# The third group's second matmul in seven half products, with its helpers moved to other engines and places

## The chip, the cores and the metric

The kernel runs on one core of a Trainium2 chip. The metric is the device time of one execution in microseconds, the median of three runs. A profile is of one such execution: its span is counted from the first to the last instruction that the profiler saw, and lies a little below the time of the same execution.

## The reference

The input x has 8 sequences of 4224 tokens with 192 channels. First comes a causal convolution over tokens with 7 taps; the taps are a softmax of a weight per head, and each of 8 heads has 24 channels. Its result is normalised per token and goes through two matrix products with a ReLU between them, and is added to that product.

```python
w = softmax(weight)                                   # (8 heads, 7 taps)
out = einsum('hk,bskhg->bshg', w, windows_of(x, 7))   # causal, padded with zeros
mu, var = out.mean(-1), out.var(-1)
xn = (out - mu) / sqrt(var + 1e-6) * g_ln
y = out + maximum(xn @ w_ch1, 0) @ w_ch2              # 192 -> 768 -> 192
```

All is in float32 (the two weight matrices arrive as doubles and are put together from their two words on the chip).

## The kernel before

**Groups.** Each of the 128 partitions holds tokens, and the tokens are cut into 18 groups: group 0 has 6 tokens per partition, group 1 has 8 (the left over tokens of all sequences), group 2 has 10, and groups 3 to 17 have 16 each. The list `groups` stands on line 70. All order is written out by hand; each engine runs its instructions in the order of the program, and waits are put in where data asks for them.

**What happens to a group g.** `load_x` (L132) brings x into one of two buffers. `first_tap` (L369) writes tap 0 times x to y on ScalarE. From group 4 on, `second_tap` (L382) writes tap 1 times x to a tile tb, also on ScalarE, and two transfers on the POOL queue (L392) add tb to y in memory, an accumulating transfer for each half of the tokens. `conv` (L397) adds the other taps on VectorE, an instruction per tap and head (L403). `transpose` (L408) brings y to channel-major form in yt, 32 x 32 blocks at a time. `moments` (L425) takes mean and variance per token (L434), and `root` (L436) makes 1/sqrt(var) of them with 19 small instructions on GpSimd. `store_y` (L472) writes y to the output, where `add_to_out` (L886) later adds the scaled second product by accumulating transfers on the POOL queue.

**The two products.** The first product, `up` (L525), and the second, `down` (L738), use 32-wide tiles of TensorE, four at a time. For groups 0 to 2 each is done in full: 144 matrix products, two instructions each. From group 3 on both are cut into halves along both dimensions and done in seven half products with sums before and after (Winograd's form of Strassen's algorithm): `up_mixed` (L587) and `down_fast` (L789). That needs sums of the quarters of w1 and w2 (`sums_of_quarters`, L555), sums of the quarters of yt (`sums_of_y`, L569, two on VectorE and two on GpSimd), and half sums of the hidden tile between the products (`half_sum`, L770, and `lower_sum`, L777). `product` (L801) is one half product: for three column blocks, 12 matrix products each, then a copy from PSUM by ScalarE (L812), and then the next few pieces of other ScalarE work from the list `work`.

**Order around the change.** The loop over groups (L973) does for g = 0, 1, 2: load of x for g + 2, `up(g)`, taps and transpose of group g + 1 on VectorE, the first taps of g + 2, `down(g)`, and `park(g)` (ScalarE copies the product out of PSUM, L870). At g = 1 it also finishes group 0 and 1 (`finish`, L919, transposes back), makes the roots of groups 0 to 2 (L1005, L1008), and all four sums of w2 on VectorE (L1006). At g = 2 VectorE makes the four sums of w1 (L1012) and the sums of yt for group 3 (L1013). While `up(2)` runs, ScalarE scales groups 0 and 1 (L884) and the POOL queue adds them to the output. The hidden tile is one large room in SBUF, shared by all groups; a group of fewer tokens uses the first part of it in the full form.

In `down_fast`, the first four half products need only the hidden tile, `lower_sum` and two sums of w2. Then VectorE makes three triples of half sums, (1,1), (0,0) and (0,1), which the last three half products read. The first triple can start when the third product has been read.

Of the kernel before, what the change touches and what calls it, by code (L numbers as in the profile page):

```python
# [16 lines left out]
def kernel(  # L17
# [59 lines left out]
    fast[NG - 1] = J - 5  # L77
    NFAST = max(fast.values())
# [53 lines left out]
    def load_x(g, queue=nc.sync):  # L132
# [3 lines left out]
        flat = t.rearrange("p j d -> p (j d)")  # L136
        if b is None:
# [14 lines left out]
        if b:  # L152
# [7 lines left out]
            nc.gpsimd.memset(t[0:1, 0:PAD, :], 0.0)  # L160
# [221 lines left out]
    def second_tap(g, heads=(0, H)):  # L382

        n = groups[g][2]
        if heads[0] == 0:
            tb[g] = bpool.tile([P, J, D], F32, tag="tb", name=f"tb{g}")
# [3 lines left out]
        if heads[1] == H:  # L390
            for j1, j2 in ((0, n // 2), (n // 2, n)):
                nc.gpsimd.dma_start(  # L392
                    out=y[g][:, j1:j2].rearrange("p j d -> p (j d)"),
                    in_=tb[g][:, j1:j2].rearrange("p j d -> p (j d)"), accum_op=ALU.add,
                )
# [99 lines left out]
    def evict_up(g, f, src):  # L495
# [4 lines left out]
        elif width(g) == C:  # L500
            dst = ht[g][:, :, f // FC, f % FC].rearrange("p h q j t -> p q h (j t)")
# [22 lines left out]

    def up(g):  # L525
# [3 lines left out]
        scaled = (0, 1) if g == 2 else ()  # L529
        hidden_tile(g)  # L530
        for f in range(NF):
# [8 lines left out]
            if 1 <= f <= 4:  # L540
                for s in scaled:
                    m = groups[s][2]
                    scale(s, m * (f - 1) // 4, m * f // 4)
                    if f % 2 == 0:
                        add_to_out(s, m * (f - 2) // 4, m * f // 4)


# [7 lines left out]
    def sums_of_quarters(dst, b11, b12, b21, b22):  # L555
        d0, d1, d2, d3 = dst
        for v, a, b in ((d2, b12, b22), (d0, b12, b11), (d1, b22, d0), (d3, b21, d1)):
            nc.vector.tensor_tensor(v, a, b, op=ALU.subtract)
# [28 lines left out]
    def up_mixed(g, ahead, pending):  # L587
# [79 lines left out]
        next(ahead)  # L667

# [120 lines left out]
    def down_fast(g, work):  # L789
# [32 lines left out]
        if g + 2 < NG:  # L822
# [4 lines left out]
        product(0, a[:, 0, 0], b[0], c11, True, 3)  # L827
        product(1, a[:, 1, 0], w2sums[:, 2], c22, True, 2)
        product(1, a[:, 1, 1], w2sums[:, 3], c21, False, 2)
        product(1, a[:, 0, 1], b[2], None, True, 3)  # L830
        if g + 1 < NG:
            transpose(g + 1)
        half_sum(g, (1, 1), (1, 1), (1, 0), ALU.add)
# [12 lines left out]
        if g + 1 < NG:  # L846
            sums_of_y(g + 1, nc.gpsimd)
            moments(g + 1)
        else:
            finish_fast(g, 0, flat, cs, parts)  # L850
# [35 lines left out]
    def add_to_out(g, j1, j2):  # L886
# [3 lines left out]
        for ps, rows in rows_of_out(g, j1, j2) if j2 else ():  # L890
            nc.gpsimd.dma_start(  # L891
# [166 lines left out]
```

## Time and profile before

| | us |
|---|---|
| median of 3 runs | 962.1 (960.88 to 962.82) |
| the profiled execution | 960.25 |
| its span | 958.5 |
| TensorE busy / VectorE busy / ScalarE busy / GpSimd busy | 948.6 / 895.8 / 686.6 / 260.9 |
| second product of group 0, 1, 2 in the chain of waits | 11.84, 15.68, 19.52 |
| second product of groups 3 to 16, each | 27.44 |
| first product of groups 3 to 16, each | 27.96 |

The busy time of an engine is the time in which at least one of its instructions runs. The chain of waits is found from the last instruction backwards: at each step it names what that instruction waited for. What stands in it has set the end; what does not stand in it was hidden. A group of instructions has its line in the kernel, the engine, the operation, the tile written and the tile read, the shapes, and a mean duration; consecutive instructions of one engine overlap a little, so their pace is read from a stretch of the timeline, as its length over their count.

### The profile page before, as it was taken

What the parts mean: (1) busy time and instruction counts of PE and PEld (TensorE: products, weight loads), DVE (VectorE), ACT (ScalarE), POOL (GpSimd) and SP (SyncE); (2) the same over time, 40 slices, a digit from 0 to 9 for tenths busy, and PEclk for the clock granted to TensorE, in tenths of its full rate; (3) what the DMA queues carried; (4) which work ended last, traced back from release to release, by engine and by line L of the source; (5) the groups of instructions that cost most, each with busy time, mean ns of one, the idle gap of its engine ahead of it and who ended that gap; (6) DMA issues with size and microseconds to landing.
All of it is one profiled execution on the core that took longest, in us unless ns stands there. A gap on an engine that the chain in (4) does not pass through costs nothing.

```text
span 958.5 us, 38499 instructions
## 1 busy us (share of the span) xinstructions
PE 948.6 (99%) x17274; PEld 719.5 (75%) x17274; DVE 895.8 (93%) x1510; ACT 686.6 (72%) x1139; POOL 260.9 (27%) x399
## 2 busy tenths in 40 slices
PE   8999999999999999999999999999999999999997
PEld 7886596776869687786958678686867768586787
DVE  8999998999999999999999999999989999999667
ACT  6625578596877959687796958778695877866461
POOL 1005311612135131422216131341315221161400
PEclk9999999999999999999999999999999999999999
DMA  8243887679697887969788796978879697767241
GB/s 221 79 155 112 180 207 216 146 151 265 134 260 142 235 173 158 249 123 276 136 240 163 178 234 118 281 136 243 158 186 216 120 280 141 179 132 129 53 83 68
DMA packets 28394, 166.69 MB, mean 174 GB/s; under 512 B 3397, under 2 KB 4294, under 8 KB 22215
## 3 DMA queue, kind: packets, MB, share of 16 engines
q0 software_dynamic: 21568, 100.94, 55.0%
q1 hardware_dynamic: 6656, 63.31, 17.9%
q8 instruction: 135, 2.21, 0.9%
q14 instruction: 29, 0.24, 0.1%
q10 hardware_dynamic: 6, 0.00, 0.0%
HBM read 38.93 MB, written 50.33 MB: 93 GB/s over the span
## 4 chain that ended last, share of the span: by engine, by line
PE 97%; ACT 1%; DMA 1%; DVE 0%; SPq 0%; issue 0%; ACTq 0%
PE ps L519 48%; PE ps L806 42%; PE ps L753 6%; DMA xg<-in_x_dram 1%; PE ps L322 1%; ACT w L360 0%; ACT room L618 0%; DVE y L898 0%; ACT spare L241 0%; ACT y L378 0%; PE ps L335 0%; SPq L215 0%; ACT room L509 0%; PE ps L350 0%; SPq L210 0%
## 5 line engine op out<-in xcount | busy, mean ns | idle before, releaser
L403 DVE SCALAR_TENSOR_TENSOR y<-xg,taps,y 128x384 f32<-128x384 f32 (+3 forms) x734 | 367.9, 577 | 1.8 <-issue 1.6
L519 PE MATMUL ps<-yt,w 32*128 32x256 f32 (+2 forms) x4104 | 235.7, 379 | 0.4 <-ACT room L509 0.4
L806 PE MATMUL ps<-room,w2sums 128*32 128x256 f32 (+1 forms) x4320 | 235.9, 375 | 0.0
L618 ACT COPY room<-ps 128x1024 f32<-128x1024 f32 (+1 forms) x135 | 175.0, 1296 | 77.2 <-PE ps L519 76.0
L519 PEld LDWEIGHTS ps<-yt,w 32*128 32x128 f32 x4104 | 204.2, 185 | 26.5 <-issue 9.0
L806 PEld LDWEIGHTS ps<-room,w2sums 128*32 128x32 f32 x4320 | 140.5, 110 | 89.7 <-ACT room L631 4.9
L806 PE MATMUL ps<-room,w 128*32 128x256 f32 (+1 forms) x3240 | 181.0, 375 | 0.4 <-issue 0.4
L773 DVE TENSOR_TENSOR room<-room 128x1024 f32<-128x1024 f32 (+1 forms) x135 | 151.6, 1196 | 21.2 <-PE ps L806 20.0
L806 PEld LDWEIGHTS ps<-room,w 128*32 128x32 f32 x3240 | 104.8, 110 | 68.7 <-DVE room L624 5.0
L519 PE MATMUL ps<-ysums,w1sums 32*128 32x256 f32 x2160 | 124.9, 379 | 0.0
L519 PEld LDWEIGHTS ps<-ysums,w1sums 32*128 32x128 f32 x2160 | 108.7, 185 | 11.2 <-ACT room L618 3.6
L812 ACT COPY cs<-ps 128x256 f32<-128x256 f32 (+1 forms) x180 | 66.0, 369 | 42.6 <-PE ps L806 42.6
L884 ACT ACTIVATE ot<-ot,r 128x192 f32<-128x192 f32 x232 | 93.8, 462 | 0.0
L631 ACT ACTIVATE room<-room 128x1024 f32<-128x1024 f32 (+1 forms) x89 | 92.1, 1071 | 0.0
L891 POOL DMA_DIRECT2D out_dram<-ot x40 | 34.2, 1086 | 194.6 <-ACT ot L884 115.7
L378 ACT ACTIVATE y<-xg,taps 128x384 f32<-128x384 f32 (+3 forms) x141 | 72.8, 611 | 9.0 <-DVE st L434 7.6
L434 DVE BATCH_NORM_STATS2 st<-y 128x6 f32<-128x192 f32 x264 | 70.2, 344 | 0.0
L519 PE MATMUL ps<-yt,w1sums 32*128 32x256 f32 x1080 | 65.1, 379 | 0.0
L812 ACT COPY room<-ps 128x256 f32<-128x256 f32 (+1 forms) x90 | 33.6, 373 | 43.9 <-PE ps L806 42.4
L519 PE MATMUL ps<-ysums,w 32*128 32x256 f32 x1080 | 64.5, 376 | 0.0
L618 ACT ACTIVATE room<-ps 128x1024 f32<-128x1024 f32 (+1 forms) x30 | 43.6, 1454 | 27.6 <-PE ps L519 27.6
L389 ACT ACTIVATE tb<-xg,taps 128x384 f32<-128x384 f32 x112 | 61.9, 635 | 0.0
(109 smaller groups left out, 895.3 us busy)
## 6 DMA issues: line engine op xcount, KB each, us to landing
xg<-in_x_dram SPq DMA_DIRECT2D x15, 2112.0 KB, 19.2
room<-room POOLq DMA_DIRECT2D x45, 512.0 KB, 5.3
out_dram<-ot POOLq DMA_DIRECT2D x29, 768.0 KB, 9.5
y<-tb POOLq DMA_DIRECT2D x28, 768.0 KB, 11.4
out_dram<-y SPq DMA_DIRECT2D x13, 1536.0 KB, 10.8
room<-parts_cs POOLq DMA_DIRECT2D x28, 512.0 KB, 6.6
room<-parts_tb POOLq DMA_DIRECT2D x14, 1024.0 KB, 7.6
xg<-in_x_dram SPq DMA_DIRECT2D x1, 1536.0 KB, 8.0
```

The costliest lines, as they stand in the source:

```text
L378: nc.scalar.mul(y[g][:, 0:n, cs], xg[g][:, 0:n, cs], taps[:, h, 0:1])
L389: nc.scalar.mul(tb[g][:, 0:n, cs], xg[g][:, 1 : 1 + n, cs], taps[:, h, 1:2])
L403: nc.vector.scalar_tensor_tensor(out=y[g][:, 0:n, cs], in0=t[:, k : k + n, cs], scalar=taps[:, h, k : k + 1], in1=y[g][:, 0:n, cs], op0=AL ...
L434: nc.vector.bn_stats(out=sums[g][:, j, :], in_=y[g][:, j, :])
L519: nc.tensor.matmul(banks[:, q, i * w : i * w + w], right[rows, c, P * i : P * i + P], left[rows, :, c, :], start=(first and c == 0 and i = ...
L618: nc.scalar.activation(dst, src, AF.Relu) if relu else nc.scalar.copy(dst, src)
L631: nc.scalar.activation(c, c, AF.Relu)
L753: nc.tensor.matmul(bank[C * q : C * q + C, 0:w], w2[:, f, C * c : C * c + C], left, start=(f == 0), stop=(f == NF - 1),)
L773: nc.vector.tensor_tensor(a[:, *dst, f], a[:, *left, f], a[:, *right, f], op=op)
L806: nc.tensor.matmul(dst[C * q : C * q + C, 0:w], right[:, f, C * c : C * c + C], left[:, f, q], start=(first and f == PAIR), stop=(f == PAI ...
L812: nc.scalar.copy(to[:, c], dst[:, 0:w].rearrange("p (j t) -> p j t", t=t))
L884: nc.scalar.mul(ots[g][:, j, :], ots[g][:, j, :], rstd[g][:, j : j + 1])
```

## The change

Group 2 (10 tokens) now has `fast[2] = 10`: its second product goes through `down_fast`, in seven half products whose tiles are 160 columns wide, where `down` used 320. Its first product stays as it was, but its result goes to the quarters of the hidden tile. With that come:

- Group 2 gets a second tap on ScalarE and accumulating transfers (three, of 4, 4 and 2 tokens), and VectorE's taps of it start at tap 2. Its tb lies in the tile ys.
- Group 3 gets a second tap for six of the eight heads. Its tb lies in the last part of the shared room, so it has to be read before `up(2)` fills that part; the four transfers move pieces of 144 channels. VectorE's taps of group 3 are cut into four stretches.
- The sums of w1 and w2 go from VectorE to GpSimd, each let in by a small memset on VectorE (`let_in`) that stands where transposes or moments follow. Only one sum of w1 stays on VectorE.
- All accumulating transfers of y and of the output, in all groups but group 1's output, move four tokens each (`add_second_tap`, `add_to_out`), where they moved half a group.
- The load of x for group 3 is issued before the stores of y of group 1, that of group 4 from the POOL queue, and that of group 5 behind a memset in `down_fast(2)`.
- The root of group 2 runs inside the first product of group 3; `store_y(3)` is issued there too. Scaling of groups 0 and 1 and the taps of groups 3 and 4 on ScalarE are placed between the evictions by a function `between`.

```diff
+    fast[2] = groups[2][2]
...
-    def load_x(g, queue=nc.sync):
+    def load_x(g, queue=nc.sync, pad=True, gate=False):
...
+        if gate:
+            nc.vector.memset(t[0:1, 0:1, 0:1], 0.0)
...
+        elif g == 2:
+            part = upool.tile([P, 3 * HJ * CH * C], F32, tag="ys", name="tb2")
+            tb[g] = part[:, 0 : n * D].rearrange("p (j d) -> p j d", d=D)
+        elif g == 3:
+            tb[g] = room[:, (NF * NQ * C - D) * J :].rearrange("p (j d) -> p j d", d=D)
...
-            for j1, j2 in ((0, n // 2), (n // 2, n)):
-                nc.gpsimd.dma_start(
-                    out=y[g][:, j1:j2].rearrange("p j d -> p (j d)"),
-                    in_=tb[g][:, j1:j2].rearrange("p j d -> p (j d)"), accum_op=ALU.add,
-                )
+            add_second_tap(g)
+
+    def add_second_tap(g, upto=H):
+        n = groups[g][2]
+        for js in (slice(j, min(j + 4, n)) for j in range(0, n, 4)):
+            ends = [v[:, js, 0 : upto * GRP] for v in (y[g], tb[g])]
+            if upto == H:
+                ends = [v.rearrange("p j d -> p (j d)") for v in ends]
+            nc.gpsimd.dma_start(out=ends[0], in_=ends[1], accum_op=ALU.add)
...
+    def between(g, f):
+
+        if g == 1 and f > 2:
+            second_tap(3, heads=[(0, 2), (2, 5), (5, 6)][f - 3])
+        elif g == 2:
+            if f == 0:
+                scale(0, 0, groups[0][2])
+                add_to_out(0, 0, groups[0][2])
+                nc.gpsimd.memset(xg[4][0:1, 0:PAD, :], 0.0)
+            elif f < 3:
+                m = groups[1][2]
+                scale(1, m * (f - 1) // 2, m * f // 2)
+                if f == 2:
+                    add_to_out(1, 0, m)
+            else:
+                first_tap(4, heads=[(0, 3), (3, 6), (6, 7)][f - 3])
...
-    def sums_of_quarters(dst, b11, b12, b21, b22):
-        d0, d1, d2, d3 = dst
-        for v, a, b in ((d2, b12, b22), (d0, b12, b11), (d1, b22, d0), (d3, b21, d1)):
-            nc.vector.tensor_tensor(v, a, b, op=ALU.subtract)
+    def let_in(tile):
+
+        nc.vector.memset(tile[0:1, 0:1, 0:1], 0.0)
+
+    def sums_of_quarters(dst, a, b):
+        nc.gpsimd.tensor_tensor(dst, a, b, op=ALU.subtract)
...
         next(ahead)
+        if g == 3:
+            store_y(g, nc.gpsimd)
...
+        behind = (1, 1, 1, 1) if g == 2 else (3, 2, 2, 3)
...
             transpose(g + 1)
+            if g == 2:
+                b11, b12 = quarters_of_w1()[0:2]
+                nc.vector.tensor_tensor(b12, b12, b11, op=ALU.subtract)
...
             sums_of_y(g + 1, nc.gpsimd)
+            if g == 2:
+                load_x(5, gate=True)
             moments(g + 1)
...
+            step = 4 * D if groups[g][0] is not None else (j2 - j1) * D
+            for d0 in range(0, (j2 - j1) * D, step):
+                d1 = min(d0 + step, (j2 - j1) * D)
+                nc.gpsimd.dma_start(out=rows[:, d0:d1], in_=src[:, d0:d1], accum_op=ALU.add)
...
-    results, pending = None, iter(())
+    results, pending = None, root(2)
...
-        if g + 2 < NG:
+        if g + 2 < NG and g not in (1, 2, 3):
             load_x(g + 2)
...
+        if g == 0:
+            early = CH * C // GRP
+            conv(1, heads=(0, early))
+            transpose(1, 0, CH)
+            conv(1, heads=(early, H))
+            transpose(1, CH, NC)
+            load_x(3)
+            store_y(1)
+            let_in(w1sums[:, 1])
+            moments(0)
+            moments(1)
+            first_tap(2)
+            second_tap(2)
+            sums_of_quarters(w1sums[:, 1], w12, w22)
+            sums_of_quarters(w2sums[:, 2], b12, b22)
+            next(root(0, True))
+        elif g == 1:
+            conv(2, 2)
+            transpose(2)
+            store_y(2)
+            first_tap(3)
+            add_second_tap(3, 6)
+            let_in(w1sums[:, 0])
+            sums_of_quarters(w1sums[:, 0], w11, w1sums[:, 1])
+            load_x(4, nc.gpsimd, pad=False)
+        elif g == 2:
+            conv(3, 2, 5, heads=(0, 6))
+            lower_sum(2)
+            conv(3, 5, K, heads=(0, 6))
+            let_in(w1sums[:, 2])
+            sums_of_quarters(w1sums[:, 2], w21, w1sums[:, 0])
+        if g < 2:
             down(g)
             park(g)
             if g == 1:
+                moments(2)
                 finish(0)
+                conv(3, heads=(6, H))
+                let_in(w2sums[:, 0])
                 finish(1)
+                sums_of_quarters(w2sums[:, 0], b12, b11)
+                sums_of_quarters(w2sums[:, 1], b22, w2sums[:, 0])
+                sums_of_quarters(w2sums[:, 3], b21, w2sums[:, 1])
             continue
```

On VectorE the order from group 1's last transpose on is thus: moments of groups 0 and 1, 40 taps of group 2, its transpose, moments of group 2, group 0's transposes back, 12 taps of group 3, group 1's transposes back, 18 taps, three lower sums of group 2, 12 taps, the transpose of group 3, the sum of w1, nine half sums, three additions, two sums of yt, moments of group 3.

## The prediction

> **What bounds the kernel now.** I read the totals of the engines first, then the chain of waits in order of time, then the timelines of VectorE, ScalarE and the two DMA queues from 20 to 190 us, and last the groups of instructions by shape, for prices.
>
> ```profile
> PE 948.6 (99%) x17274; PEld 719.5 (75%) x17274; DVE 895.8 (93%) x1510; ACT 686.6 (72%) x1139; POOL 260.9 (27%) x399
> PE 97%; ACT 1%; DMA 1%; DVE 0%; SPq 0%; issue 0%; ACTq 0%
> ```
>
> The chain itself, with start, length and instruction:
>
> ```profile
> 64.84 15.68 PE ps L753 x288
> 80.52 19.59 PE ps L519 x288
> 100.11 19.52 PE ps L753 x288
> 119.63 27.82 PE ps L519 x504
> 147.45 27.44 PE ps L806 x504
> ```
>
> TensorE is 97% of the chain, and from 31 us on its stages follow each other without a gap. So time is won only by less TensorE work, and each wait that reaches TensorE is lost in full. The third group's second product is the piece of 19.52 us at 100.11. VectorE is the engine that can spoil a gain:
>
> ```profile
> 49.39 1.62 DVE L434 BATCH_NORM_STATS2 st<-y 128x6 f32<-128x192 f32 x6
> 50.92 18.28 DVE L403 SCALAR_TENSOR_TENSOR y<-xg,taps,y 128x240 f32<-128x240 f32 x48
> 69.31 2.18 DVE L414 STREAM_TRANSPOSE yt<-y 128x1920 f32<-128x1920 f32 x1
> 81.36 25.49 DVE L403 SCALAR_TENSOR_TENSOR y<-xg,taps,y 128x384 f32<-128x384 f32 x48
> 159.04 10.31 DVE L773 TENSOR_TENSOR room<-room 128x1024 f32<-128x1024 f32 x9 [1.05 <-PE ps L806]
> ```
>
> These rows are start, time, engine, line. VectorE runs without idle time from 31.6 to 143.5 us; a step gives 18.28/48 = 0.381 us per tap of 240, 25.49/48 = 0.531 per tap of 384. The last row is the half sums of a seven-product group: they start when the third product ends, and the fifth product needs the first three.
>
> **What the Trainium skill says.** (1) "DMA: Bandwidth & Descriptors", section "Queues, rings and completion order": each DMA engine goes round between its queues and drains a whole packet of descriptors before it switches. The trace agrees: a store issued by SP at 154.53 moves nothing until 158.9, when the eight 6144-byte pieces per engine of an earlier POOL transfer are through. (2) "SBUF — State Buffer", "Who interferes with whom": a GpSimd instruction that reads SBUF and a VectorE instruction with two SBUF inputs exclude each other for a whole instruction; one with a single input does not contend. The trace shows the harmless half: the 768-element sums on POOL take 1.83 us beside the moments, whose pace stays 0.26. (3) "GPSIMD Engine Reference", "Side-by-side cycle accounting": tensor_tensor is 1.96 times slower there; here 1832 against 949 ns, 1.93. (4) "DMA: Bandwidth & Descriptors", "Why small descriptors are slow (HBM only)": between SBUF and SBUF small pieces aren't penalised. No run here shows pieces of 576 bytes.
>
> **The change part by part.**
>
> *TensorE.* Removed: 288 matmul instructions of 320 columns, 19.52 us. Added: 7 x 72 = 504 of 160 columns. The last group has this shape:
>
> ```profile
> L753 PE MATMUL ps<-room,w 128*32 128x160 f32 x288 | 10.0, 299 | 0.0
> L581 POOL TENSOR_TENSOR ysums<-yt 128x768 f32<-128x768 f32 x14 | 25.6, 1832 | 44.4 <-PE ps L806 39.5 <-DVE ysums L580 5.0
> L576 DVE TENSOR_TENSOR ysums<-yt 128x768 f32<-128x768 f32 x15 | 14.2, 949 | 0.0
> ```
>
> The 10.0 us there hold waits at its end; in its even stretch a bank of 48 took 1.63 us, 0.0340 each. 504 x 0.0340 = 17.14 us; saved 2.38. One product is 2.45 us, so with no wait the fifth starts at 100.11 + 4 x 2.45 = 109.90, and the next group at 117.25 instead of 119.63. No other TensorE work changes.
>
> *VectorE, if no transfer is late.* From 49.39: 14 moments at 0.26 = 3.66, 53.05. Forty taps of 240 (eight went to ScalarE and an accumulating transfer) 15.3, 68.4; transpose 2.1, 70.5; 10 moments 2.6, 73.1; group 0's transposes 1.6, 74.7; 12 taps of 384 6.35, 81.05; group 1's transposes 2.05, 83.1; 18 taps 9.5, 92.6; three half sums of 640 (1.135 us at 1024 and 0.80 at 704 give 0.735) 2.2, 94.8; 12 taps 6.35, 101.2; transpose 3.3, 104.5; one sum of 1152 1.4, 105.95. The third product ends at 107.4, so VectorE has 1.45 us in hand, and some 0.2 more because three half sums (2.2) are shorter than a product (2.45). After that: nine half sums, three additions of about 0.25, two of 0.95 bring it to about 117; 16 moments and the finish of group 2 (3.9) let group 4's taps begin near 125.2, 7.9 us after TensorE's start of the group, against 6.3 before and 7.05 in the steady groups. The product that is closed at 145.0 waited 1.46 us for TensorE before, which covers that.
>
> *ScalarE.* Added: 8 taps of 240 (3.1 us, 41.1 to 44.2; the copies it pushes back have until 49.1), six second taps of group 3 between the evictions of group 1 (0.53 each, they fill gaps of 1.57), 18 short copies for 6. In the seven products it does a copy of some 0.2 and a tap of 0.52 per 0.82 us: nothing. Group 4's first tap at 95 needs x of group 4, now loaded from POOL's queue behind a sum; I get it landed and padded near 91.
>
> *POOL's sums.* Three of 1152 (1.83 x 1152/768 = 2.75 us) and four of 288 (about 0.8). Where they fall beside moments and transposes they cost nothing; beside taps VectorE waits up to a whole sum. The second of 1152 stands behind four DMA issues that wait for ScalarE until 70.65 (0.55 us apart in the trace): 72.9 to 75.6, so 0.9 us of taps are held if VectorE is on time, none if it is 1 us late. The three sums of w2 (2.4 us) overhang group 1's transposes (2.05) by 0.3.
>
> *Group 2's new accumulating transfer.* This is the price that decides. ScalarE's taps end at 44.25; an accumulating transfer moved its first piece 1.4 us after issue (834.1 to 835.5), so 45.7. Three transfers: twice 8 pieces of 3072 bytes per engine (0.263 each, between 0.196 for 2304 and 0.340 for 4096) and 8 of 1536 (0.139): 2.1 + 2.1 + 1.1, ending at 51.2. But x of group 3 moves:
>
> ```profile
> 48.48 5.00 SPq L475 DMA_DIRECT2D out_dram<-y  x8
> 53.58 0.37 SPq L148 DMA_DIRECT2D xg<-in_x_dram  x1
> ```
>
> SP issued the stores first; now the load goes at 48.48 and its eight pieces per engine of 0.629 us (5.0) arrive at 49.4, while the second transfer is being drained (until 49.9). By (1) the load comes before the third transfer: 49.9 + 5.0 + 1.1 = 56.0, and 0.5 to be seen: VectorE's taps start at 56.5, not 53.05. Bounds: nothing if the three are drained first; 58.5 if the stores behind the load go ahead too. I take 3.5 us of lateness.
>
> *Sum.* 3.5 + 0.3 of late VectorE = 3.8: the half sums start at 109.75, three end at 112.0, the fifth product at 112.05 instead of 109.90, a wait of 2.15. Span 958.5 - 2.38 + 2.15 = 958.3; with the 1.75 us around the span (960.25 - 958.5) 960.0. The median of the runs shown, 962.1, is 1.85 above that execution, so I forecast 961.9.
>
> *Four tokens at a time.* y and out transfers double in number: four more issues per group, 2.2 us of a POOL that is 27% busy. Pieces of 3072 cost 2 x 0.263 where 6144 cost 0.479, 0.75 us more per 1.5 MB. In the steady groups y's transfers land 3 to 4 us before their taps, so nothing; if that cover were gone, up to 1.5 us a group. The later load of group 5 (near 117, used after 145), the root of group 2 (POOL, 121 to 131, read at about 136) and the later store of y of group 3 are hidden.
>
> **Rivals.** A: the wait goes out at about the old level (above), 961.9. B: the three transfers are drained before the load; VectorE is late by about 1.2 (POOL's sums), within its 1.65: the whole 2.38 stays, 959.8. For it: they are issued 4 us ahead. Against: the trace's switch at 158.9. C, slower: group 3's transfer from the shared tile goes in pieces of 576 bytes, 2048 pieces or 128 per engine. A line through 1536 to 8192 bytes gives some 0.078 us a piece, 10 us, landed near 84 with a store between: VectorE wants it at 86.6. The price of a 1536-byte piece, 0.139, is the upper bound: landed at 72.1 + 17.8 + 2.5 = 92.4, lateness 9.3, wait 7.6, 967.3. It decides from 0.115 a piece (landed at 89.3: slower by 2.0). Below: the price can't fall under the 0.036 at which the line meets zero bytes, and then A stands.
>
> **How the numbers follow.** A measurement here can tell 0.2%, 1.92 us, from no change. A 0.47, B 0.31, C with lesser late stalls of its sign 0.22. A reaches from 960.3 to 963.5, nearly all within 0.2%, a little on each side; B mostly beyond it. Range 959.4 to 965.0. Faster 0.33, within 0.2% 0.42, slower 0.25.
>
> **What would show it.** In the changed profile: 504 instructions of 160 columns at 0.034 us; a wait of VectorE before the first tap of 240 of 3 to 4 us, ended by the transfer from tb; a gap of about 2 us before the fifth product, released by the half sums; POOL's sum of 1152 beside moments. Wrong, if TensorE shows no gap near 110 (B), if group 3's taps wait at 87 (C), or if steady groups gain gaps.

## The result and the profile after

| | before | after |
|---|---|---|
| median over the runs of one comparison, us | 960.8 (959.7 to 962.9, 22 runs) | 962.5 (961.3 to 966.6, 22 runs) |
| ratio after to before, 95% interval | | 1.0019 (1.0011 to 1.0026) |
| profiled execution, its span, us | 960.25, 958.5 | 963.98, 962.1 |
| TensorE's stages: second product of group 2 | 19.52 | 19.03 |
| first product of group 3 | 27.82 | 28.07 |
| second product of group 3 | 27.44 | 30.53 |

The kernel became 1.7 us slower by the medians of the two. The three stages are measured from the start of a stage's first matrix product to the start of the next stage's, in the two profiled executions. They add up to 2.85 us more. Every later stage is equal (27.96 and 27.44 us), but for four stages that start between 676 and 761 us and are 0.2 to 0.6 us longer, since TensorE stalls in them; the kernel before has such a stage too (0.95 us longer, from 646), and they fall differently in each kernel's profiled execution. The profiled execution after lies above its median, so its span shows more than the medians do.

The totals of the engines and the shares of the chain, by engine, of the changed kernel:

```profile
PE 948.9 (99%) x17490; PEld 725.1 (75%) x17490; DVE 894.9 (93%) x1510; ACT 696.0 (72%) x1165; POOL 340.5 (35%) x473
PE 92%; DMA 3%; ACT 2%; POOL 1%; DVE 1%; issue 0%; SPq 0%; ACTq 0%; POOLq 0%; DVEq 0%
```

TensorE's share of the chain has fallen from 97% to 92%: other engines now release it somewhere. TensorE's own timeline of group 2's second product shows the first of these places (start, time, engine, line, tiles, shape and count; in brackets the idle time before it and what ended it):

```profile
99.94 2.65 PE L834 MATMUL ps<-room,w 128*32 128x160 f32 x72
102.41 5.07 PE L834 MATMUL ps<-room,w2sums 128*32 128x160 f32 x144
107.30 2.63 PE L834 MATMUL ps<-room,w 128*32 128x160 f32 x72
111.43 5.17 PE L834 MATMUL ps<-room,w2sums 128*32 128x160 f32 x144 [1.50 <-DVE room L801]
```

Four products take 2.45 us each, as expected, and then TensorE is idle for 1.50 us until VectorE's half sums are there; from matrix product to matrix product the gap is 1.80 us. VectorE's timeline, from group 2's taps to the half sums:

```profile
53.35 15.26 DVE L418 SCALAR_TENSOR_TENSOR y<-xg,taps,y 128x240 f32<-128x240 f32 x40 [0.32 <-DMA y<-tb]
...
75.02 8.82 DVE L418 SCALAR_TENSOR_TENSOR y<-xg,taps,y 128x384 f32<-128x384 f32 x12
...
85.77 10.13 DVE L418 SCALAR_TENSOR_TENSOR y<-xg,taps,y 128x384 f32<-128x384 f32 x18
...
107.86 1.32 DVE L867 TENSOR_TENSOR w<-w 128x1152 f32<-128x1152 f32 x1
109.10 6.70 DVE L801 TENSOR_TENSOR room<-room 128x640 f32<-128x640 f32 x9
```

Group 2's taps waited only 0.32 us for their accumulating transfers. But 12 taps of group 3 took 8.82 us where 12 others take 6.4, and 18 took 10.13 where 9.6 is their pace. At that time POOL did this:

```profile
69.67 5.24 POOL L410 DMA_DIRECT2D y<-room  x4 [9.71 <-ACT y L382]
72.78 4.81 POOL L584 TENSOR_TENSOR w1sums<-w,w1sums 128x1152 f32<-128x1152 f32 x1
```

The four issues with pieces of 576 bytes took 1.31 us each, so the sum of w1 behind them came to run beside the taps. One tap of the twelve took 3.00 us (their median is 0.605). The difference is nearly the length of the sum by itself, 2.65 us.

The second place is group 3's second product. These are POOL's queue, then ScalarE's timeline, then the chain there (start, length, what):

```profile
133.85 0.89 POOL L611 DMA_DIRECT2D room<-room  x1
134.45 0.85 POOL L490 DMA_DIRECT2D out_dram<-y  x1
135.37 1.79 POOL L611 DMA_DIRECT2D room<-parts_cs  x2
```

```profile
145.80 1.06 ACT L657 ACTIVATE room<-room 128x1024 f32<-128x1024 f32 x1 [2.08 <-DMA room<-parts_cs]
148.91 1.06 ACT L657 ACTIVATE room<-room 128x1024 f32<-128x1024 f32 x1 [2.05 <-DMA room<-parts_cs]
149.87 1.86 ACT L644 ACTIVATE room<-ps 128x2048 f32<-128x2048 f32 x1
```

```profile
133.37 0.44 POOL r L484
133.85 2.44 DMA room<-room
136.29 12.60 DMA room<-parts_cs
149.01 0.85 issue
149.87 1.86 ACT room L644
```

Read from the end: TensorE's second product waits for ScalarE's copy of the last first product (149.87). That copy stands behind two ReLUs (L657) that wait for the accumulating transfers of parts_cs. These were issued at 135.37, right behind the store of y of group 3, which moves 12288 bytes per partition on the same queue from 138 to 141.9; and the store stands behind a transfer issued at 133.85, late because the small instructions of the root of group 2 were still running in front of it. The root's last instruction (`POOL r L484`) and the transfer stand next to each other in the chain.

### The profile page after: what moved, and what is told of

Its sections match the earlier page's. It is cut to its first block, busy times and chain, and to the rows that moved or that the text cites. A ratio compares the mean times of both kernels' runs of the same rounds, so it can differ in the third digit from the quotient of the medians.

```text
span 962.1 us, 39172 instructions
## 1 busy us (share of the span) xinstructions
PE 948.9 (99%) x17490; PEld 725.1 (75%) x17490; DVE 894.9 (93%) x1510; ACT 696.0 (72%) x1165; POOL 340.5 (35%) x473
## 4 chain that ended last, share of the span: by engine, by line
PE 92%; DMA 3%; ACT 2%; POOL 1%; DVE 1%; issue 0%; SPq 0%; ACTq 0%; POOLq 0%; DVEq 0%
PE ps L534 45%; PE ps L834 43%; PE ps L781 4%; DMA room<-parts_cs 1%; DMA xg<-in_x_dram 1%; PE ps L369 1%; ACT room L644 1%; ACT room L657 0%; SPq L142 0%; DMA room<-room 0%; ACT ot L921 0%; DVE room L801 0%; POOL d L461 0%; POOL room L611 0%; DVE y L937 0%
## 5 line engine op out<-in xcount | busy, mean ns | idle before, releaser
L834 PE MATMUL ps<-room,w2sums 128*32 128x256 f32 (+2 forms) x4608 | 246.8, 370 | 2.0 <-DVE room L801 1.5
L834 PEld LDWEIGHTS ps<-room,w2sums 128*32 128x32 f32 x4608 | 148.1, 110 | 95.0 <-ACT room L657 6.2
L834 PE MATMUL ps<-room,w 128*32 128x256 f32 (+2 forms) x3456 | 189.4, 370 | 2.0 <-ACT room L657 1.9
L801 DVE TENSOR_TENSOR room<-room 128x1024 f32<-128x1024 f32 (+2 forms) x147 | 160.6, 1165 | 21.3 <-PE ps L834 21.3
L834 PEld LDWEIGHTS ps<-room,w 128*32 128x32 f32 x3456 | 111.7, 110 | 71.5 <-DVE room L650 5.0
L932 POOL DMA_DIRECT2D out_dram<-ot x69 | 59.2, 988 | 163.9 <-ACT ot L921 107.8
L410 POOL DMA_DIRECT2D y<-tb x59 | 52.5, 1386 | 150.4 <-ACT room L840 110.1
L840 ACT COPY cs<-ps 128x256 f32<-128x256 f32 (+2 forms) x192 | 70.1, 368 | 44.7 <-PE ps L834 44.7
L657 ACT ACTIVATE room<-room 128x1024 f32<-128x1024 f32 (+1 forms) x89 | 92.9, 1073 | 6.7 <-DMA room<-parts_cs 6.6
L840 ACT COPY room<-ps 128x256 f32<-128x256 f32 (+2 forms) x96 | 35.4, 368 | 50.8 <-PE ps L834 49.5
L400 ACT ACTIVATE tb<-xg,taps 128x384 f32<-128x384 f32 (+1 forms) x120 | 66.0, 626 | 0.0
```

The costliest lines, as they stand in the source:

```text
L400: nc.scalar.mul(tb[g][:, 0:n, cs], xg[g][:, 1 : 1 + n, cs], taps[:, h, 1:2])
L657: nc.scalar.activation(c, c, AF.Relu)
L801: nc.vector.tensor_tensor(a[:, *dst, f], a[:, *left, f], a[:, *right, f], op=op)
L834: nc.tensor.matmul(dst[C * q : C * q + C, 0:w], right[:, f, C * c : C * c + C], left[:, f, q], start=(first and f == PAIR), stop=(f == PAI ...
L840: nc.scalar.copy(to[:, c], dst[:, 0:w].rearrange("p (j t) -> p j t", t=t))
L932: nc.gpsimd.dma_start(out=rows[:, d0:d1], in_=src[:, d0:d1], accum_op=ALU.add)
```

## The experiments

Each was compared with the kernel before on the same chip, in 5 rounds, with 4 to 22 runs of the edited kernel (4 of x10, 5 of x11, 6 of x16, 10 of x13). The chip is not the same for all of them, so experiments are compared with each other by their ratios. TensorE's stages of each profiled execution, in us:

```
                            second, g2  first, g3  second, g3   ratio to before (95%)
before                         19.52      27.82      27.44
after                          19.03      28.07      30.53      1.0019 [1.0011, 1.0026]
x1  store moved                25.21      28.44      27.44      0.9999 [0.9987, 1.0012]
x2  sum moved                  18.16      28.52      30.04      1.0015 [0.9999, 1.0032]
x3  store and sum moved        17.92      28.79      27.43      0.9991 [0.9982, 0.9999]
x4  no root of group 2         18.97      27.90      27.44      0.9986 [0.9979, 0.9993]
x5  before + store             19.52      27.82      27.44      0.9997 [0.9988, 1.0007]
x6  before + root              19.52      27.82      27.53      1.0005 [0.9996, 1.0014]
x16 before + store + root      19.52      27.82      30.50      1.0042 [1.0028, 1.0056]
x7  x3, load behind stores     17.87      28.79      27.43      0.9997 [0.9989, 1.0006]
x8  x3, root early             21.30      27.90      27.44      1.0011 [0.9996, 1.0026]
x10 x3, root behind last sum   17.25      36.13      30.15      1.0085 [1.0072, 1.0098]
x11 x2, root behind last sum   17.25      36.69      29.45      1.0081 [1.0067, 1.0095]
x9  x3, halves everywhere      19.29      28.45      27.44      1.0013 [1.0000, 1.0025]
x12 x3, group 4 by 2 tokens    17.25      28.50      27.33      0.9969 [0.9961, 0.9977]
x13 x3, group 4 by 8 tokens    21.52      28.59      27.45      1.0023 [1.0007, 1.0038]
x14 x3, by 8 except group 4    17.90      28.72      27.44      0.9979 [0.9972, 0.9987]
x15 after, group 4 by 2        18.95      28.34      29.93      1.0022 [1.0010, 1.0033]
```

**The store of y of group 3** (x1). It leaves POOL's queue for SP's.

```diff
-        if g == 3:
-            store_y(g, nc.gpsimd)
...
             conv(3, 5, K, heads=(0, 6))
+            store_y(3)
```

> The changed kernel with one thing moved: the store of y of group 3 is issued by SP when group 3's taps are done (near 104 us, where the DMA engines of the changed kernel are idle from 106 to 110), not by POOL between the transfers room<-room and room<-parts_cs. Theory 1 (the store, 3.9 us of the POOL queue's DMA, stands ahead of room<-parts_cs and makes ScalarE's ReLU and so the second product of group 3 late): the TensorE gap of 1.9 us at 148 and the one of 0.3 at 158 go, room<-parts_cs lands near 145 instead of 148.9, time about 3 us below the changed kernel (its median 962.5, so near 959.5). Theory 2 (the root of group 2 on POOL delays the transfers): the gap stays, time within 1 us of the changed kernel. Theory 3 (the later load of group 5's x is what collides): the gap stays too.

Group 3's second product is back at 27.44, so the 3.1 us went away with the store; the median came to 960.5 us, where 959.5 was expected. But the profiled execution of this kernel (966.8 us, the slowest of its 14 runs) showed something else, on VectorE and then TensorE:

```profile
59.27 15.26 DVE L418 SCALAR_TENSOR_TENSOR y<-xg,taps,y 128x240 f32<-128x240 f32 x40 [6.81 <-DMA y<-tb]
```

```profile
114.94 7.92 PE L832 MATMUL ps<-room,w2sums 128*32 128x160 f32 x144 [4.92 <-DVE room L799]
```

This is the prediction's lost turn. Here the load of x of group 3 began to move near 51, when a third to a half of group 2's third transfer had been drained; its pieces of 1536 bytes then crept on at a tenth of the engines' time beside the 16896-byte ones until 58. The pieces of both are spread over the same seven microseconds, so the load came in between the pieces of one transfer: in this execution the eight pieces of an engine were not drained in one turn, as the prediction's point (1) has it. The stage is 25.21 us long because the idle time of 4.92 us was followed by a lower granted clock of TensorE (0.50 from 114 to 120). In the changed kernel's profile the third transfer ended near 52 and the load began then. A microsecond decides between nothing and 7 us. Of the thirteen profiles here with the load ahead of the stores this one alone shows it.

**The sum of w1** (x2, and with the store x3). It goes ahead of the late DMA issues, beside group 2's transpose.

```diff
+            let_in(w1sums[:, 0])
             transpose(2)
+            sums_of_quarters(w1sums[:, 0], w11, w1sums[:, 1])
...
             add_second_tap(3, 6)
-            let_in(w1sums[:, 0])
-            sums_of_quarters(w1sums[:, 0], w11, w1sums[:, 1])
```

> The changed kernel with the second sum of w1 on GpSimd let in before group 2's transpose and put ahead of the four transfers of group 3's second tap, so that it lies beside one-input instructions. Theory (a GpSimd sum holds VectorE's two-input taps for its whole length): the tap of 3.0 us at 75 is gone, the 12 taps take 6.35 us instead of 8.8, the wait before the fifth product of group 2 falls from 1.5 us to under 0.4, and group 3 starts near 117.7 instead of 119.05. If the wait at 148 does not shrink, time falls by about 1.3 us; if that wait grows by as much as was won, by nothing. Rival (the late part is the landing of the pieces of 576 bytes): the wait stays, since these transfers are issued 1.6 us later here.

> Both moves together. If the two losses are separate and in series: 2.4 us saved less what remains, about 4.4 us below the changed kernel, some 2.5 us below the kernel before. If one hides the other, no better than the better of the two alone.

VectorE's timeline of x2:

```profile
76.04 6.40 DVE L418 SCALAR_TENSOR_TENSOR y<-xg,taps,y 128x384 f32<-128x384 f32 x12
...
85.47 9.61 DVE L418 SCALAR_TENSOR_TENSOR y<-xg,taps,y 128x384 f32<-128x384 f32 x18 [1.03 <-DMA y<-room]
...
108.64 6.71 DVE L801 TENSOR_TENSOR room<-room 128x640 f32<-128x640 f32 x9 [0.27 <-PE ps L834]
```

The twelve taps are back at 6.40, and now VectorE waits for TensorE before the half sums: the fifth product's wait is gone. The pieces of 576 bytes, issued later here, do make the 18 taps wait 1.03 us, which stays covered. Alone the move gained nothing in the time that is clear of the noise, for group 3's wait stayed. With both moved, group 3's second product is right too; yet group 2's took 17.92, not 17.2, and the kernel is 0.9 us faster than before by the ratio, not the 2.5 us expected. Group 3's first product is 0.97 us longer than before in x3. TensorE stalls there too (0.28 us at 121.00, "issue"); what makes this up was not tested.

**Store or root?** In x4 the root of group 2 is left out, and group 0's factor is used in its place; x5 and x6 put one of the two moves into the kernel before, x16 both.

```diff
 x4:
-    results, pending = None, root(2)
+    results, pending = None, iter(())
+            rstd[2] = rstd[0]
 x16 (x5 has the store alone, x6 the root alone), against the kernel before:
+        if g == 3:
+            store_y(g, nc.gpsimd)
...
-    results, pending = None, iter(())
+    results, pending = None, root(2)
-                store_y(g + 1, nc.gpsimd)
-                next(root(2, True))
```

> The changed kernel without the root of group 2 (its 19 small GpSimd instructions are left out, and group 2 is scaled with group 0's factors). Theory 1 (the store): the transfer of c21 is issued some 4 us earlier and room<-parts_cs with it, so up to 3 us are won here as well although the store stays; with the store still 3.9 us long ahead of room<-parts_cs, I expect it to land by 145 to 147 and 1 to 3 us won. If the root plays no part: nothing won.

> The kernel before, with only the store of y of group 3 moved into the first product of group 3, on the POOL queue ahead of the two transfers of half the tokens; the root of group 2 stays where it was. Theory (store and root are each covered, and only both together make the accumulating transfers late): group 3's second product stays at 27.4 to 27.8 us and the time within 0.5 us of before. Rival (the store alone is enough: its 12288-byte pieces stand ahead of the transfers that ScalarE waits for): 2 to 3 us more in group 3's second product, ratio 1.002 to 1.003.

> The kernel before, with only the root of group 2 moved into the first product of group 3; the store of y of group 3 stays where it was. Theory (both are needed): POOL's transfer of c21 is issued some 4 us later, at about 133, the next ones at about 136, which is no later than before, and group 3's second product stays at 27.4 to 27.8 us; time within 0.5 us of before. Rival (the root alone is enough, since it holds POOL some 5 us): 2 to 3 us more in that stage.

> The kernel before with both moves and nothing else: the root of group 2 and the store of y of group 3 (POOL queue) in group 3's first product. Theory (together they make the accumulating transfers of that product late by the store's 3.9 us; each alone is covered): ScalarE waits about 2 us for them near 146, group 3's second product takes 29.5 to 31 us, ratio to before 1.002 to 1.0035. Rival (they are late only where TensorE is 2 us earlier, as in the changed kernel): 27.4 to 28.2 us, ratio under 1.001.

Without the root group 3's second product is 27.44 although the store stays. In the kernel before, each move alone changes nothing, and both together make that stage 30.50, the very stage of the changed kernel. POOL's queue with the store alone, with the root alone, and with both:

```profile
129.42 0.86 POOL L475 DMA_DIRECT2D out_dram<-y  x1
135.46 1.79 POOL L585 DMA_DIRECT2D room<-parts_cs  x2 [5.19 <-ACT parts_cs L618]
```

```profile
135.03 0.88 POOL L585 DMA_DIRECT2D room<-room  x1
136.36 1.76 POOL L585 DMA_DIRECT2D room<-parts_cs  x2 [0.45 <-ACT parts_cs L618]
```

```profile
138.03 0.88 POOL L585 DMA_DIRECT2D room<-room  x1
138.63 0.85 POOL L475 DMA_DIRECT2D out_dram<-y  x1
139.36 1.90 POOL L585 DMA_DIRECT2D room<-parts_cs  x2
```

With the store alone POOL issues it 6 us ahead of the transfers that count and then idles 5.19 us. With the root alone POOL still idles 0.45 us before them. With both, the root uses up the 6 us, and the store's data go directly ahead of the transfers. (That kernel started 3.5 us later in its execution; what counts is the order.)

**The load of x of group 3** behind the stores of y of group 1, as before the change (x7), on top of x3.

```diff
-            load_x(3)
             store_y(1)
+            load_x(3)
```

> The changed kernel with the store of y of group 3 on SP's queue, the sum of w1 beside group 2's transpose, and the load of x of group 3 put back behind the stores of y of group 1. Theory (the load meets group 2's accumulating transfers in some executions and not in others): with the load behind the stores VectorE's 40 taps of group 2 begin right after the moments, near 53, and the runs lie closer together than those of the kernel with the load ahead; median 960.2 to 960.6. If x then lands too late for ScalarE's taps of group 3 (first ones near 61), the 12 or 18 taps of group 3 wait, 0.5 to 2 us. Rival (the stores take the load's place in the race): the taps of group 2 wait here too, 2 to 6 us, in the profile.

Group 2's taps began at 54.33, directly behind the moments. The load then came too late for another engine, ScalarE:

```profile
64.67 1.12 ACT L400 ACTIVATE room<-xg,taps 128x384 f32<-128x384 f32 x2 [2.57 <-DMA xg<-in_x_dram]
```

Its copies for group 1's products stand behind this tap, and TensorE's two stages of group 1 took 0.69 and 0.26 us more. The runs lay between 960.0 and 963.0, but those of x3 between 958.3 and 963.1: whether the order narrows them is open, and by the median it gains nothing.

**The root elsewhere** (x8, x10, x11). In x8 it runs on POOL ahead of the last sum of w1, in x10 and x11 behind it.

```diff
 x8, x10, x11:
-    results, pending = None, root(2)
+    results, pending = None, iter(())
 x8:
             lower_sum(2)
+            next(root(2, True))
 x10, x11:
             sums_of_quarters(w1sums[:, 2], w21, w1sums[:, 0])
+            next(root(2, True))
```

> The changed kernel with the store of y of group 3 on SP's queue, the sum of w1 beside group 2's transpose, and the root of group 2 back ahead of group 3's first product (POOL, some 95 to 101). Theory: POOL's accumulating transfers of group 3's first product are issued as early as in the kernel before; nothing that TensorE waits for changes, since store and root are each covered alone, so the time is that of the kernel with the store moved and the sum moved, 960.2 to 960.9. Rival (the root still costs something in group 3's first product, which is 28.8 us there and 27.8 before): that stage falls to 28.0 or less and the time to 959.5 to 960.

> The changed kernel with the store of y of group 3 on SP's queue, the sum of w1 beside group 2's transpose, and the root of group 2 on POOL behind the last sum of w1 (some 104.6 to 110), where nothing waits for it; with the root ahead of that sum the sum was 5.4 us late and held one half sum for 3.2 us. Theory (the delayed sum was the whole loss there): half sums take 6.7 us again, group 2's second product 17.2 to 18.0 us, group 3's first product 27.9 to 28.8, time 959.3 to 960.6. Rival (the small instructions of the root hold VectorE's half sums one by one): the nine half sums take 8 to 9 us, the fifth to seventh products wait 1 to 2 us, 961 to 962.

> The changed kernel with only the sum of w1 beside group 2's transpose and the root of group 2 on POOL behind the last sum of w1; the store of y of group 3 stays on POOL's queue in group 3's first product. Theory (store and root are each covered alone): no wait in group 3's second product (27.4 to 27.6 us), time 959.3 to 960.6, as with the store moved too. Rival (the store's transfer of 3.9 us ahead of those that ScalarE waits for costs something by itself once TensorE is 2 us earlier): 0.5 to 3 us more in that stage.

All three theories missed in the time: the medians are 961.8, 969.5 and 968.8 us. In x8 POOL and VectorE show why:

```profile
107.32 2.66 POOL L584 TENSOR_TENSOR w1sums<-w,w1sums 128x1152 f32<-128x1152 f32 x1
```

```profile
107.44 9.10 DVE L799 TENSOR_TENSOR room<-room 128x640 f32<-128x640 f32 x9
```

The sum, 5.4 us later than in x3, held one half sum for 3.22 us, and the fifth product waited 2.17 us. Group 3's first product fell to 27.90 there, as the rival had it, but this was less than the wait cost. In x10 the small instructions of the root were the losers: beside the half sums they took 0.66 us each, and everything behind them on POOL came late:

```profile
116.96 3.57 POOL L410 DMA_DIRECT2D y<-tb  x4 [0.33 <-issue]
```

```profile
133.04 14.91 DVE L418 SCALAR_TENSOR_TENSOR y<-xg,taps,y 128x384 f32<-128x384 f32 x28 [6.56 <-DMA y<-tb]
```

Group 4's transfers were issued 8.9 us later than in x3 and VectorE waited 6.56 us for them. TensorE waited three times in group 3's first product: 1.34 us for POOL's sum of yt, 2.01 us for ScalarE and 4.33 us for VectorE. After the last wait its granted clock was 0.50 from 153 to 158, which makes the second product 30.15 us long. x11 doesn't tell store from root, since its group 3 is late anyway. But in both kernels group 2's second product took 17.25 us: the whole gain, in the two kernels where group 4's transfers didn't run beside it.

**Four tokens at a time.** x9 takes the transfers of x3 back to halves of the tokens.

```diff
-        for js in (slice(j, min(j + 4, n)) for j in range(0, n, 4)):
+        step = 4 if g < 4 else n // 2
+        for js in (slice(j, min(j + step, n)) for j in range(0, n, step)):
...
-            step = 4 * D if groups[g][0] is not None else (j2 - j1) * D
+            step = (j2 - j1) * D
```

> The changed kernel with the store of y of group 3 on SP's queue and the sum of w1 beside group 2's transpose, and with the accumulating transfers of y (from group 4 on) and of the output moving half of the tokens again, as before the change. Theory (the number of transfers is hidden in every steady group): stages of 27.96 and 27.44 us as ever, time within 0.5 us of the same kernel with transfers of four tokens, 960.1 to 961.0. Rival (each pair of transfers more costs a little at the end of a group): 1 us or more less.

It took 962.6 us, against 960.6 for x3 in its own comparison; the ratios are 1.0013 and 0.9991. So the theory, and the prediction's "nothing", were wrong in this kernel. Three more experiments separate group 4 from the rest, by the line for step (`2 if g == 4 else 4` in x12, `8 if g == 4 else 4` in x13, `8 if g > 4 else 4` and the output's halves in x14), and x15 makes x12's edit in the changed kernel alone.

> The changed kernel with the store of y of group 3 on SP's queue and the sum of w1 beside group 2's transpose, and group 4's accumulating transfers of y in two tokens each (1536-byte pieces; 3072 with four tokens). Theory (TensorE's instruction packets take turns with the pieces of these transfers, and a turn is as long as one transfer's eight pieces): the stall before the seventh product of group 2, 0.55 us with 3072-byte pieces and 1.9 with 6144, falls to 0.3 us or less, that stage takes 17.2 to 17.7 us, time 0 to 0.5 us less than with four tokens. Rival (the stall has nothing to do with pieces): 0.5 us or more of stall as before, 17.9.

> The same kernel with group 4's accumulating transfers of y alone in halves of eight tokens (6144-byte pieces); all other transfers of four tokens. Theory: the stall of TensorE before the seventh product of group 2 is 1.5 to 2.2 us, that stage takes 19 to 19.5 us, and the time is 1 to 1.8 us above that with four tokens. Rival (transfers of the steady groups made the difference): stall 0.6 or less, time as with four tokens.

> The same kernel with halves of eight tokens in all groups from 5 on and in the transfers of the output; group 4 stays at four tokens. Theory (only group 2's second product asks for instructions so fast that a long turn makes it stall; the steady groups are hidden): group 2's second product as with four tokens, 17.9 us, steady stages 27.96 and 27.44, time within 0.6 us of the kernel with four tokens. Rival (the steady groups pay now and then): 1 us or more above it, with stalls of TensorE in some stages between 600 and 800 us.

> The changed kernel with group 4's accumulating transfers of y in two tokens each, and nothing else changed. Theory (in the changed kernel the fifth product's wait of 1.8 us for the half sums gives TensorE's instructions the time to arrive, so the turn of these pieces is covered, and group 3's accumulating transfers stay late): group 2's second product about 19.0 us, group 3's about 30.5, ratio to before 1.001 to 1.003. Rival (smaller pieces help by themselves): 1 us or more below the changed kernel, ratio under 1.001.

TensorE's timeline at the seventh product of group 2 in x12 (1536-byte pieces), x3 (3072) and x13 (6144), in this order:

```profile
109.53 5.07 PE L833 MATMUL ps<-room,w2sums 128*32 128x160 f32 x144
114.42 2.63 PE L833 MATMUL ps<-room,w 128*32 128x160 f32 x72
```

```profile
109.19 5.07 PE L832 MATMUL ps<-room,w2sums 128*32 128x160 f32 x142
114.51 0.30 PE L832 MATMUL ps<-room,w2sums 128*32 128x160 f32 x1 [0.25 <-issue]
```

```profile
109.57 5.07 PE L833 MATMUL ps<-room,w2sums 128*32 128x160 f32 x142
116.80 0.30 PE L833 MATMUL ps<-room,w2sums 128*32 128x160 f32 x1 [2.17 <-issue]
```

TensorE is idle for 0, 0.25 and 2.17 us (from matrix product to matrix product the gaps are 0, 0.5 and 2.5 us), and "issue" says that the profile shows no data and no other engine that was late. x14, with 3072-byte pieces and in the same comparison as x12 and x13, has 0.22. So the size of the pieces of group 4's transfers sets this stall. The trace also has the packets of a queue that carries instructions, 16384 bytes each. Two that follow each other in this stage start at:

```
                                        packets start at       apart   one turn of the transfer
x10 no transfer of y beside them        107.10   110.48         3.4
x12 1536-byte pieces                    107.34   111.42         4.1      8 x 0.140 = 1.1
x3  3072-byte pieces                    106.93   112.24         5.3      8 x 0.253 = 2.0
x13 6144-byte pieces                    107.44   114.44         7.0      8 x 0.479 = 3.8
```

Each distance is the 3.4 of x10 plus 0.7, 1.9 or 3.6: up to one turn of the accumulating transfer, 8 pieces on each DMA engine. The first of the two packets starts 7.5 to 7.7 us after the stage in all four; the second 10.9, 11.7, 12.9 and 14.7 us after it. (In x11, also without such a transfer, one starts after 10.8 us.) This fits what the Trainium skill says in "DMA: Bandwidth & Descriptors", section "Queues, rings and completion order": an engine drains a whole packet of descriptors from one queue before it goes to the next. The prediction used that sentence for loads and stores; here the packets of instructions wait in the same way. Group 2's second product asks for them fastest: 504 products and 504 weight loads in 17.25 us, 58 a us, where the steady second product has 37 a us (504 of each in 27.44). The profile of x3 counts 137 packets of 16384 bytes for 39176 instructions, 286 each; at 58 a us one lasts about 4.9 us, by this estimate. Distances of 5.3 and 7.0 us are longer by 0.4 and 2.1 us, and TensorE stalled; 4.1 is shorter, and it didn't. The trace doesn't name the engine that a packet is for. That they are TensorE's is read from this pace and from the stalls: the effect of the piece size is shown, this path of it is argued.

x14 has long pieces in all groups from 5 on and in the output, and is as fast as x3 or faster: the steady groups don't feel the piece size. On one chip x12, x14 and x13 took 957.5, 959.1 and 963.3 us. x15 shows that in the changed kernel itself smaller pieces are worth nothing: the fifth product still waits 1.8 us from matrix product to matrix product, and TensorE's timeline shows no stall by "issue" behind it.

**The version that beats both** is x12: store on SP's queue, sum beside the transpose, group 4 by two tokens. It took 957.5 us (956.7 to 961.3, 21 runs), ratio to before 0.9969 [0.9961, 0.9977]. That is 3.0 us, of which the three stages of its profile account for 1.7; where the rest was won was not traced. Group 3's first product is still 0.68 us longer than before: VectorE's taps of group 4 wait 1.14 us for the root of group 2 on POOL, and TensorE then 0.29 us for VectorE.

## Why the prediction was right or wrong

- **The TensorE term was right.** 17.14 us was forecast for the seven products without a wait; x10, x11 and x12 have 17.25, so 2.27 us were to be had, not 2.38. The changed kernel itself kept 0.49 of them.
- **The failed step is the sentence of the working that puts the other moves at nothing: "The later load of group 5 [...], the root of group 2 [...] and the later store of y of group 3 are hidden."** It priced each move alone, and each alone is hidden indeed (x5, x6). Together on POOL's queue they cost 3.06 us of TensorE in group 3's second product (x16: 30.50 against 27.44), and the changed kernel paid 3.09. It was this that turned a small gain into a loss. The prediction gave no time for the transfers of parts_cs that ScalarE's ReLU reads, though they go through POOL's queue behind both moves.
- **The wait before the fifth product came, from another cause.** Forecast 2.15 us, measured 1.50 of idle time. The step "the load comes before the third transfer", 3.5 us, didn't happen in the profiled execution of the changed kernel; it did in x1's, with 6.81. In its place stood the term "0.9 us of taps are held" by POOL's sum: it was 2.4 (8.82 against 6.40), since the four issues ahead of it took 5.24 us and not 4 x 0.55. The Trainium skill's "SBUF — State Buffer", "Who interferes with whom", which the prediction cites, calls the ports that the two engines share an exclusive lock, and the tap of 3.00 us agrees. The sums of w2 held 0.5 instead of 0.3. Lateness is thus 2.4 + 0.5 + 0.3 = 3.2 us, less 1.65 in hand 1.55, near the measured 1.50. So rival B's condition was met (the three transfers were drained before the load), and B's time wasn't. That the wait has about the forecast size is luck: one lateness stood in for another.
- **Rival C was rightly low.** A piece of 576 bytes took 0.089 us in the changed kernel, nearer the 0.078 of the line than the 0.115 from which it decides; no tap of group 3 waited for it. What these pieces did cost was POOL's time to issue them, 1.31 us for each transfer, which the prediction had put at 0.55.
- **"Four tokens at a time [...] nothing"** holds in the steady groups (x14), and fails for group 4 once the other waits are mended: x13 against x12 is 963.3 against 957.5 us. In the changed kernel itself only the step from four tokens to two was run (x15, no gain), not the step back to halves. The prediction thought of it as transfer time; the runs show it in stalls of TensorE by "issue".
- **The time came out near, the sign didn't.** The forecast was 0.2 us under the median shown then, the result is 1.7 us above the kernel before. That 961.9 lies close to 962.5 is luck: the median shown, of three runs, was 1.3 us above that of 22 runs, which hides most of the miss. That group 2's gain and its wait nearly balance was as forecast (19.03 against 19.52 us); group 3's 3 us were not in the sum, nor in any rival: the slower one was sought at group 3's transfer from the shared room.

## What to carry to other kernels

Work moved onto a queue is priced with everything else that the same change moves there, up to the next instruction that someone waits for: two moves that were free alone cost 3.06 us together here. A helper instruction that shares a lock with the busy engine belongs ahead of every DMA issue that can be late, not behind one: moving one sum ahead of four issues took away the fifth product's wait. And where a stage is cut into more and shorter instructions, look at what the DMA queues do beside it: in these runs the packets of instructions came later, the longer the pieces of the transfers beside them were.

## What the runs showed of the hardware

- Issuing a transfer on POOL costs more when it has more pieces: four issues in a row took 5.24 us where each transfer has 512 pieces of 576 bytes (1.31 each), and 3.57 us where each has 128 pieces of 3072 bytes (0.89 each).
- A stall of TensorE can cost twice. After 2.17 us of idle time in x13 and x8, and after the longer waits of x1 and x10 (4.92 and 4.33 us), the granted clock fell to half; after 1.50 and 1.90 us (changed kernel), 1.62 us (x9) and 2.01 us (x10) it didn't. The windows of x13, with TensorE's clock, the DMA share and GB/s in the last three columns:

```profile
114.00:117.00 3.00, 0.83 (x23) 0.50 (x19) 2.97 (x10) 0.19 (x1) 0.45 (x1) 1.00 0.98 198
117.00:119.00 2.00, 2.00 (x45) 1.96 (x47) 2.00 (x9) 0.59 (x2) 1.92 (x2) 0.70 1.06 244
119.00:121.50 2.50, 2.50 (x39) 1.94 (x34) 2.47 (x9) 0.40 (x2) 1.26 (x1) 0.56 0.98 419
```

  The stage took 21.52 us, where 19 to 19.5 had been expected, and 4.3 more than without the stall, of which the gap from matrix product to matrix product is 2.5 and most of the rest the lower clock. The Trainium skill ("TensorE: Matmul & The Clock Gate", "Part 1: The HAM clock gate (the "warmup" mystery)") gives an idle window of about 3.4 us before the clock falls; here 2.17 us of idle time were enough.
- Of two engines with a common lock either can lose. POOL's sum of 2.65 us held one VectorE instruction for all its length (3.00 instead of 0.605, 3.22 instead of 0.81); in x10 VectorE's nine half sums, one behind the other, took 6.76 us, as long as without the root beside them (6.71 in x3), and POOL's small instructions stretched from 0.21 to 0.66.
